# Finished w_out words left in PSUM, k and q copies on ScalarE, routing in program order

## The chip, the cores and the metric

The kernel runs on one core of one Trainium2 chip. The metric is the device time of one execution in microseconds (us); lower is better. TensorE (PE) does the matrix products, VectorE (DVE), ScalarE (ACT) and GpSimd (POOL) the elementwise work, SyncE (SP) issues most DMAs. Every engine takes its own instructions in a fixed order; engines wait for each other by semaphores.

## The reference

Three stages follow each other. `x` of one stage is the output of the stage before.

```python
# attention with a decay: 4 batches, 8 heads, 576 positions, 64 wide
scores = q @ k.T / 8 + cum[:, None] - cum[None, :]     # cum = cumsum(log f), causal
attn   = softmax(scores);  x = attn @ v                # 2304 tokens x 512
# first mixture: a dense product with a gate
h = x @ w_in                                            # 512 -> 2048
x = (h * clip(h + 3, 0, 6) / 6) @ w_out                 # 2048 -> 512
# second mixture: each token goes to one of 8 experts
e = argmax(x @ w_gate); c = softmax(x @ w_gate)[e] * sigmoid((x @ w_output_gate)[e])
out = c * (relu(x @ w1[e]) @ w2[e])                     # 512 -> 1024 -> 512
```

Inputs and output are float32.

## The kernel before

Float32 accuracy comes from pairs: every operand is split into a 16-bit high word and a 16-bit low word (`hi`, `lo`), and each product is three matmuls (hi by hi, hi by lo, lo by hi). The splits are what DVE, ACT and POOL are busy with.

**Conversion of w_in and w_out.** `w_in` and `w_out` arrive as 64-bit words. `conv_raw` (from line 638) turns 32 pieces into pairs, 16 of `w_in` ("wi") and then 16 of `w_out` ("wo"). DVE makes the float32 word in three integer operations (lines 651, 653, 655): the first two work in a PSUM tile `cv`, of which there is one, the third writes an SBUF tile `w32` (in the profile `w`), of which there are two. ACT copies it to the high word (line 658), and the low word is a subtraction (line 659), on POOL for `wi` and on DVE for `wo`.

**Attention.** A "piece" is 128 or 64 positions of several heads of k or q. `split_kq` (line 206) makes high and low words, a DMA transposes them, and a copy of the 64 high rows goes into the second operand of the score products: line 246 for k (`K2`, `K2t`), line 269 for q (`Q2`). Pieces 0 to 3 use TensorE transposes and a POOL copy instead, so the copies of lines 246 and 269 run from the fifth piece on. DVE then scales and reduces the scores (line 335, 361; `nm` is the row minimum), ACT exponentiates (369), ACT and DVE or POOL split the result (386, 387), a DMA transposes it (398), PE multiplies it with v (421 to 436), and DVE divides (444 to 462).

**First mixture.** Six chunks of 384 tokens. `moe1_steps` does the product with `w_in` (line 688), the gate (692 ACT, 695 DVE, 696 ACT, 700 DVE or POOL) and the product with `w_out` (line 711). Chunk c runs on PE between the attention units of later tokens. After each chunk `gate_steps` computes the routing of its tokens.

**The order.** Most instructions are placed by a scheduler, which simulates the engines and picks by priority; attention has priority 200 above the rest, conversions 500. Inside `tc.manual_schedule(engines=...)` the named engines keep the order of the program. In the kernel before only the last part, `round_` (line 1145 on), is in program order on PE, ACT and DVE.

**Between the two mixtures.** The tokens of experts 0 and 1 found in the first 15 blocks are gathered early, into rows that live in the freed `w_in` tile (`wi`), and `expert1` and `expert2` (lines 969 to 995) can run for them, 192 and 48 matmuls. Meanwhile the table of the remaining tokens is made: `rank_onehot` on DVE (line 931, `R`), `table` on PE (line 909, 36 matmuls) and DVE (913 to 922, `ids`), an indirect gather on POOL (943, `xg`), and a DMA transpose into `xs` (946). `round_` starts with `expert1` of expert 0 on `xs`. In `round_` the float32 weights of later experts stream in three buffers `stw` (line 859), are split by ACT (871) and DVE (872), and feed PE.

Of the kernel before, what the change touches and what calls it, by code (L numbers as in the profile page):

```python
# [11 lines left out]
I32 = mybir.dt.int32  # L12
AF = mybir.ActivationFunctionType
# [5 lines left out]
P = 128  # L19
# [39 lines left out]
def attention_moe_kernel(ctx: ExitStack, tc: tile.TileContext, q, k, v, f, w_in, w_out,  # L59
                         w_gate, w_og, w1, w2, out):  # L60
    nc = tc.nc
# [3 lines left out]
    E, _, F2 = w1.shape  # L65
# [13 lines left out]
    ps_mm = ctx.enter_context(tc.tile_pool(name="ps_mm", bufs=3, space=PSUM))  # L79
# [5 lines left out]
    stp = stage_ctx.enter_context(tc.tile_pool(name="stp", bufs=1))  # L85
# [146 lines left out]
    def prep_k(i):  # L232
        b, r, hs, (nh, n), cs = piece(i)
        if i < PE_PIECES:
            g, hh = cs.start // 256, hs.start // 4
            split_transposed("k", i, *([t[a:a + 64, hh, 2 * g + c] for c in range(2)]
                                       for t, a in ((K1, 0), (K1, 64), (K2, 0))))
            return
        src = split_kq("k", i)
        if n == 1:  # L240
            k1, k2 = K1t, K2t
        else:
            g = cs.start // 256
            k1, k2 = (t[:, hs.start // 4, 2 * g:2 * g + 2].rearrange("p c h j -> p (c h) j") for t in (K1, K2))
        nc.sync.dma_start_transpose(out=k1, in_=src)
        nc.vector.tensor_copy(out=k2[0:64], in_=k1[0:64])

    def prep_q(i):
        r = piece(i)[1]
        if i < PE_PIECES:  # L250
            q1 = ap1.tile([P, 8, 128], F16, tag="q1", name="q1", bufs=3)
            q2 = Q2[i % 3]
            q_t[i] = q1, q2
            cols = lambda t, a: [t[a:a + 64, :, c * 64:c * 64 + 64].rearrange("p (g h) j -> p g h j", g=2)
                                 for c in range(2)]
            split_transposed("q", i, cols(q2, 0), cols(q1, 0), cols(q1, 64))
            return
        src = split_kq("q", i)
        q1 = ap1.tile([P, 8, 128], F16, tag="q1", name="q1", bufs=3)
        if r == 64:  # L260
            nc.sync.dma_start_transpose(out=q1[:, :, 0:r], in_=src)
        else:
            for half in range(2):
                nc.sync.dma_start_transpose(
                    out=q1[:, half * 4:half * 4 + 4].rearrange("p h (c j) -> p (h c) j", c=2),
                    in_=src[half * 64:half * 64 + 64])
        q2 = Q2[i % 3]
        q_t[i] = q1, q2
        nc.vector.tensor_copy(out=q2[0:64, :, 0:r], in_=q1[64:128, :, 0:r])

    def q_cols(b, h, qb):

# [346 lines left out]
    WL = 2048  # L619
# [20 lines left out]
    def conv_raw(nm, i):  # L640

        if nm == "wi":
            hi, lo = (wi[:, x, :, i * P:i * P + P] for x in range(2))
        else:
            d, g4 = divmod(i, 4)
            hi, lo = (wo[:, x, 4 * g4:4 * g4 + 4, d * P:d * P + P] for x in range(2))
        w = raws.pop((nm, i)).rearrange("p (n t) -> p n t", t=2)

        t = stp.tile([P, WL // 4], I32, tag="w32", name="w32", bufs=2)
        tp = ps_cv.tile([P, WL // 4], I32, tag="cv", name="cv")  # L650
        nc.vector.tensor_scalar(out=tp, in0=w[:, :, 1], scalar1=3, scalar2=0x3FFFFFFF,
                                op0=ALU.logical_shift_left, op1=ALU.bitwise_and)
        nc.vector.scalar_tensor_tensor(out=tp, in0=w[:, :, 1], scalar=-0x40000000, in1=tp, op0=ALU.bitwise_and,
                                       op1=ALU.bitwise_or)
        nc.vector.scalar_tensor_tensor(out=t, in0=w[:, :, 0], scalar=29, in1=tp, op0=ALU.logical_shift_right,
                                       op1=ALU.bitwise_or)
        tf = t.bitcast(F32).rearrange("p (a b) -> p a b", a=4)
        last_act.append(nc.scalar.activation(out=hi, in_=tf, func=AF.Copy).ins)
        (nc.gpsimd if nm == "wi" else nc.vector).tensor_tensor(out=lo.bitcast(BF16), in0=tf, in1=hi, op=ALU.subtract)
# [219 lines left out]
    def count_rounds():  # L879

        ps = ps_mm.tile([P, 512], F32, tag="mm", name="mm")
        nc.tensor.matmul(ps[:, 0:E], lhsT=allone, rhs=ohsum[:, NB], start=True, stop=True)
        mx = mp2.tile([P, 1], F32, tag="cmx", name="cmx")
        more = mp2.tile([P, 8], F32, tag="more", name="more")
        nc.vector.tensor_reduce(out=mx, in_=ps[:, 0:E], axis=AX.X, op=ALU.max)
        nc.vector.tensor_tensor(out=more, in0=mx.to_broadcast([P, 8]), in1=thr, op=ALU.is_gt)
        nc.vector.tensor_reduce(out=mx, in_=more, axis=AX.X, op=ALU.add)
        nc.vector.tensor_copy(out=nrounds, in_=mx)
        nc.vector.tensor_copy(out=cnt, in_=ps[:, 0:E])
# [66 lines left out]
    def expert1(e, ps_pool, blocks):  # L956

        W1, (xs, o) = wts[e, 0], xs_t[e, blocks[0]]
        hT, ho = h_t[e, blocks[0]]
        w = len(blocks) * P  # L960
        hs = slice(ho, ho + w)
        for m in range(F2 // P):
            ps = ps_pool.tile([P, 512], F32, tag="mm", name="mm")
            i = 0
            for j in range(KD):
                for a, b2 in ((0, 0), (0, 1), (1, 0)):
                    l = W1[:, a, j, m * P:(m + 1) * P]
                    r = xs[:, b2 * KD + j, o:o + w]
                    nc.tensor.matmul(ps[:, 0:w], lhsT=l.bitcast(BF16) if a else l, rhs=r.bitcast(BF16) if b2 else r,  # L969
                                     start=i == 0, stop=i == 3 * KD - 1)  # L970
                    i += 1
            nc.scalar.activation(out=hT[:, m, 0, hs], in_=ps[:, 0:w], func=AF.Relu)  # L972
            nc.vector.scalar_tensor_tensor(out=hT[:, m, 1, hs].bitcast(BF16), in0=ps[:, 0:w], scalar=0.0,  # L973
                                           in1=hT[:, m, 0, hs], op0=ALU.max, op1=ALU.subtract)
            yield
# [25 lines left out]
    def run(g, n=1):  # L1001

        last = None
        for _ in range(n):
            r = next(g, "end")
            last = r or last
            if r == "end":
                break
        return last
# [121 lines left out]
            pass  # L1131
    run(wg_, 4 * KD + 1 - nw)
    count_rounds()
    for i in range(NBL, NB):
        rank_onehot(R, i, P, CAP)
    table(R, P, const, ps_mm, (1, 2), NB)

    for e in range(2):
        for _ in expert1(e, ps_mm, (0,)):
            pass  # L1140
    for e in range(2):
        for _ in expert2(e, None, ps_mm, (0,), wi[:, 1, e, 0:2 * DM].bitcast(F32)):
            pass
# [48 lines left out]
                for _ in expert2(e, xp, ps_mm, (2,)):  # L1192
                    pass

    ET = mybir.EngineType
    with tc.manual_schedule(engines={ET.PE, ET.Activation, ET.DVE}):
        round_(True)
    more = nc.values_load(nrounds[0:1, 0:1], min_val=0, max_val=NT // CAP)
    RA = xp.tile([P, NB, CAP], F16, name="RA")
    with tc.For_i(0, more, 1):  # L1200
# [35 lines left out]
```

## Time and profile before

| | us |
|---|---|
| median of 3 runs | 835.37 (833.76 to 836.37) |
| profiled execution, its own time | 831.17 |
| its span, first to last instruction | 829.5 |
| PE busy | 746.0 |
| DVE busy | 486.3 |
| ACT busy | 427.3 |
| POOL busy | 314.1 |
| mean granted TensorE clock | 0.962 of 2.4 GHz |

PE is busy for nine tenths of the span, so the span is PE's work plus the time in which PE has nothing to do or runs at the lower of its two clock levels. The readings are therefore made by stretch: how much PE idles in it, which wait ends that idle time, and how full the engine is that it waited for.

### The profile page before, as it was taken

What the parts mean: (1) busy time and instruction counts of PE and PEld (TensorE: products, weight loads), DVE (VectorE), ACT (ScalarE), POOL (GpSimd) and SP (SyncE); (2) the same over time, 40 slices, a digit from 0 to 9 for tenths busy, and PEclk for the clock granted to TensorE, in tenths of its full rate; (3) what the DMA queues carried; (4) which work ended last, traced back from release to release, by engine and by line L of the source; (5) the groups of instructions that cost most, each with busy time, mean ns of one, the idle gap of its engine ahead of it and who ended that gap; (6) DMA issues with size and microseconds to landing.
All of it is one profiled execution on the core that took longest, in us unless ns stands there. A gap on an engine that the chain in (4) does not pass through costs nothing. (4 is left out here: it accounts for less than half of the span.)

```text
span 829.5 us, 16702 instructions
## 1 busy us (share of the span) xinstructions
PE 746.0 (90%) x6166; PEld 480.1 (58%) x6177; DVE 486.3 (59%) x1302; ACT 427.3 (52%) x879; POOL 314.1 (38%) x388
## 2 busy tenths in 40 slices
PE   4745998889899989998999999999889999999993
PEld 2533455545566645665665656666769665667641
DVE  7998999838852865158723777760313555554510
ACT  4864776557754774256733655550113555454510
POOL 9546777656744463256522500000131322210010
PEclk9986999979999999998999999999899999999997
DMA  8758789999995684479623847612463899795410
GB/s 247 218 184 190 173 186 236 214 129 164 174 169 115 137 153 83 72 119 168 109 50 71 144 130 237 187 41 51 78 147 86 249 275 276 221 266 206 149 39 28
DMA packets 263779, 127.96 MB, mean 154 GB/s; under 512 B 214658, under 2 KB 247522, under 8 KB 263684
## 3 DMA queue, kind: packets, MB, share of 16 engines
q1 hardware_dynamic: 251860, 105.20, 58.1%
q0 software_dynamic: 4960, 15.73, 5.6%
q10 hardware_dynamic: 6864, 5.80, 2.5%
q8 instruction: 54, 0.88, 0.5%
q14 instruction: 41, 0.34, 0.2%
HBM read 71.52 MB, written 10.08 MB: 98 GB/s over the span
## 5 line engine op out<-in xcount | busy, mean ns | idle before, releaser
L688 PE MATMUL mm<-xT,wi 128*128 128x384 f16 (+1 forms) x1152 | 211.9, 332 | 9.1 <-DMA xT<-xn 4.9
L711 PE MATMUL mm<-g,wo 128*128 128x384 f16 (+1 forms) x1152 | 201.8, 328 | 0.4 <-DVE hr L695 0.4
L688 PEld LDWEIGHTS <-wi 128*128 128x128 f16 (+1 forms) x1152 | 111.0, 99 | 88.8 <-issue 21.5
L711 PEld LDWEIGHTS <-wo 128*128 128x128 f16 (+1 forms) x1152 | 111.7, 98 | 74.4 <-issue 3.8
L969 PEld LDWEIGHTS <-W 128*128 128x128 f16 (+1 forms) x1344 | 102.8, 101 | 15.2 <-issue 6.8
L369 ACT ACTIVATE ms<-ms,nm 128x512 f32<-128x512 f32 (+4 forms) x144 | 79.5, 579 | 55.5 <-DVE nm L335 30.5
L872 DVE TENSOR_TENSOR W<-stw,W 128x1024 bf16<-128x1024 f32 x64 | 77.7, 1224 | 50.6 <-ACT W L871 50.2
L387 POOL TENSOR_TENSOR pn<-ms,pn 128x384 bf16<-128x384 f32 (+1 forms) x80 | 83.0, 1044 | 62.2 <-ACT pn L386 53.4
L969 PE MATMUL mm<-xs,W 128*128 128x256 f16 (+3 forms) x1152 | 96.8, 246 | 5.9 <-DMA xs<-xg 3.6
L988 PE MATMUL mm<-W,hT 128*128 128x512 f16 (+1 forms) x422 | 93.8, 379 | 1.1
L871 ACT ACTIVATE W<-stw 128x1024 f16<-128x1024 f32 x64 | 66.8, 1054 | 45.4 <-DMA stw<-in_moe_w_dram 42.9
L335 DVE CUSTOM_DVE_ANT_1 ms<-sc,mask 128x128 f32<-128x128 f32 (+3 forms) x128 | 58.9, 485 | 24.6 <-PE sc L288 13.9
L988 PEld LDWEIGHTS <-hT 128*128 128x128 f16 (+1 forms) x432 | 41.9, 98 | 50.9 <-issue 1.6
L696 ACT ACTIVATE g<-hr 128x384 f16<-128x384 f32 x96 | 49.9, 520 | 41.2 <-DVE hr L695 40.6
L700 DVE TENSOR_TENSOR g<-hr,g 128x384 bf16<-128x384 f32 x80 | 53.8, 673 | 25.7 <-ACT g L696 25.5
L695 DVE SCALAR_TENSOR_TENSOR hr<-hr,mm 128x384 f32<-128x384 f32 x96 | 52.6, 548 | 16.1 <-ACT hr L692 15.4
L973 DVE SCALAR_TENSOR_TENSOR hT<-mm,hT 128x128 bf16<-128x128 f32 (+1 forms) x96 | 32.6, 355 | 47.9 <-ACT hT L972 43.3
L288 PE MATMUL sc<-K,q 128*128 128x256 f16 (+3 forms) x192 | 49.1, 300 | 12.8 <-DVE nm L335 9.1
L692 ACT ACTIVATE hr<-mm,bias 128x384 f32<-128x384 f32 x96 | 54.5, 568 | 11.5 <-PE mm L688 10.1
L995 POOL DMA_INDIRECT out_dram<-y,ids x18 | 20.1, 1115 | 96.4 <-ACT y L994 56.1
L421 PE MATMUL pv<-vt,pt 128*128 128x65 f16 x320 | 42.0, 199 | 15.6 <-DVE xs L446 9.5
L943 POOL DMA_INDIRECT xg<-rows,ids x22 | 24.9, 1130 | 70.7 <-DMA xs<-xg 63.7
(186 smaller groups left out, 1128.3 us busy)
## 6 DMA issues: line engine op xcount, KB each, us to landing
stw<-in_moe_w_dram SPq DMA_DIRECT2D x64, 512.0 KB
wo<-in_moe_w_in_dram SPq DMA_DIRECT2D x16, 512.0 KB
raw<-in_moe_w_out_dram ACTq DMA_DIRECT2D x11, 512.0 KB
rows<-rw POOLq DMA_DIRECT2D x15, 256.0 KB, 4.0
ldk<-in_k_dram SPq DMA_DIRECT2D x14, 256.0 KB
ldq<-in_q_dram SPq DMA_DIRECT2D x14, 256.0 KB
ldv<-in_v_dram SPq DMA_DIRECT2D x13, 256.0 KB
g<-in_moe_w_out_dram SPq DMA_DIRECT2D x3, 512.0 KB
```

The source lines that it names most:

```text
L335: nc.vector.tensor_tensor_reduce(out=pairs(ms[:, off:off + w]), in0=ps[:, 0:w].rearrange("p (c j) -> p c j", c=2), in1=pairs(mask[:, 640 - ...
L369: nc.scalar.activation(out=ms[:, off:off + w], in_=ms[:, off:off + w], func=AF.Exp, scale=-1.0, bias=nm[:, i:i + 1])
L387: nc.gpsimd.tensor_tensor(out=lo.bitcast(BF16), in0=ms[:, 0:N], in1=hi, op=ALU.subtract)
L688: nc.tensor.matmul(ps[:, 0:w], lhsT=l.bitcast(BF16) if a else l, rhs=r.bitcast(BF16) if b2 else r, start=i == 0, stop=i == 3 * KD - 1)
L692: nc.scalar.activation(out=hr, in_=ps[:, 0:w], func=AF.Relu, bias=bias3)
L695: nc.vector.scalar_tensor_tensor(out=hr, in0=hr, scalar=6.0, in1=ps[:, 0:w], op0=ALU.min, op1=ALU.mult)
L700: either.tensor_tensor(out=g[:, m, 1, 0:w].bitcast(BF16), in0=hr, in1=g[:, m, 0, 0:w], op=ALU.subtract)
L711: nc.tensor.matmul(ps[:, 0:w], lhsT=l.bitcast(BF16) if a else l, rhs=r.bitcast(BF16) if b2 else r, start=i == 0, stop=i == 3 * NF - 1)
L871: nc.scalar.activation(out=hi, in_=sts[i], func=AF.Copy)
L872: nc.vector.tensor_tensor(out=lo.bitcast(BF16), in0=sts[i], in1=hi, op=ALU.subtract)
L969: nc.tensor.matmul(ps[:, 0:w], lhsT=l.bitcast(BF16) if a else l, rhs=r.bitcast(BF16) if b2 else r, start=i == 0, stop=i == 3 * KD - 1)
L988: nc.tensor.matmul(ps, lhsT=l.bitcast(BF16) if a else l, rhs=r.bitcast(BF16) if b2 else r, start=i == 0, stop=i == 3 * NF2 - 1)
```

## The change

Three edits. (1) In `conv_raw`, for `w_out` only, the third DVE operation writes into the PSUM tile `cv` in place of an SBUF tile, and ACT and DVE read the finished word there. (2) The copies of lines 246 and 269 are ACT activations in place of DVE copies. (3) Program order on PE, ACT and DVE begins earlier: two steps of expert 0's first product, the one-hot rows and the table, then the rest of the first products of experts 0 and 1, their second products, and then `round_`.

```diff
-        nc.vector.tensor_copy(out=k2[0:64], in_=k1[0:64])
+        nc.scalar.activation(out=k2[0:64], in_=k1[0:64], func=AF.Copy)
...
-        nc.vector.tensor_copy(out=q2[0:64, :, 0:r], in_=q1[64:128, :, 0:r])
+        nc.scalar.activation(out=q2[0:64, :, 0:r], in_=q1[64:128, :, 0:r], func=AF.Copy)
...
-        t = stp.tile([P, WL // 4], I32, tag="w32", name="w32", bufs=2)
         tp = ps_cv.tile([P, WL // 4], I32, tag="cv", name="cv")
...
+        t = stp.tile([P, WL // 4], I32, tag="w32", name="w32", bufs=2) if nm == "wi" else tp
         nc.vector.scalar_tensor_tensor(out=t, in0=w[:, :, 0], scalar=29, in1=tp, op0=ALU.logical_shift_right,
                                        op1=ALU.bitwise_or)
...
+    ET = mybir.EngineType
+    first = [expert1(e, ps_mm, (0,)) for e in range(2)]
+    manual = ctx.enter_context(ExitStack())
+    manual.enter_context(tc.manual_schedule(engines={ET.PE, ET.Activation, ET.DVE}))
+    run(first[0], 2)
     for i in range(NBL, NB):
         rank_onehot(R, i, P, CAP)
     table(R, P, const, ps_mm, (1, 2), NB)
-    for e in range(2):
-        for _ in expert1(e, ps_mm, (0,)):
-            pass
+    for g_ in first:
+        run(g_, F2 // P)
...
-    with tc.manual_schedule(engines={ET.PE, ET.Activation, ET.DVE}):
-        round_(True)
+    round_(True)
+    manual.close()
```

The scheduler reacts to edits 1 and 2: from the first chunk on the rows of PE, DVE and ACT stand in another order. By the end of the product with `w_out` of chunk 1, the program before has issued 172 score matmuls (lines 288, 355, 356) and the changed one 202; in the middle of the product with `w_in` of chunk 3 both have issued 296.

On DVE, the second and third pieces of `w_out`. Before (`w_853` and `w_979` are two SBUF words):

```order
L653 SCALAR_TENSOR_TENSOR cv<-raw,cv 128x512
L246 COPY K2t<-K1t 64x512
L695 SCALAR_TENSOR_TENSOR hr<-hr,mm 128x384
L655 SCALAR_TENSOR_TENSOR w_853<-raw,cv 128x512
L651 TENSOR_SCALAR cv<-g 128x512
L269 COPY Q_1_89<-q_1051 64x8x64
L659 TENSOR_TENSOR wo<-w_853,wo 128x4x128
L653 SCALAR_TENSOR_TENSOR cv<-g,cv 128x512
L695 SCALAR_TENSOR_TENSOR hr<-hr,mm 128x384
L655 SCALAR_TENSOR_TENSOR w_979<-g,cv 128x512
```

And now:

```order
L652 SCALAR_TENSOR_TENSOR cv<-raw,cv 128x512
L656 SCALAR_TENSOR_TENSOR cv<-raw,cv 128x512
L696 SCALAR_TENSOR_TENSOR hr<-hr,mm 128x384
L660 TENSOR_TENSOR wo<-cv,wo 128x4x128
L650 TENSOR_SCALAR cv<-g 128x512
L696 SCALAR_TENSOR_TENSOR hr<-hr,mm 128x384
L652 SCALAR_TENSOR_TENSOR cv<-g,cv 128x512
```

The two copies are gone from DVE, and the first operation of a piece stands behind the subtraction of the piece before it, where it stood ahead of it.

On ACT, the same stretch. Before:

```order
L310 ACTIVATE vt_91<-ldv 128x8x64
L214 ACTIVATE kp<-ldk 128x8x64
L696 ACTIVATE g<-hr 128x384
L658 ACTIVATE wo<-w_853 128x4x128
L692 ACTIVATE hr<-mm,bias_86 128x384
L214 ACTIVATE qp<-ldq 128x8x64
```

And now:

```order
L310 ACTIVATE vt_91<-ldv 128x8x64
L246 ACTIVATE K2t<-K1t 64x512
L214 ACTIVATE kp<-ldk 128x8x64
L697 ACTIVATE g<-hr 128x384
L693 ACTIVATE hr<-mm,bias_86 128x384
L269 ACTIVATE Q_1_89<-q_1046 64x8x64
L214 ACTIVATE qp<-ldq 128x8x64
```

Each copy stands directly ahead of the split of the next piece (line 214).

On PE, where `round_` begins (`wi` are the early tokens, `xs` the ones gathered last). Before:

```order
L969 LDWEIGHTS W_7248
L969 MATMUL mm<-wi,W_7248 128x128
L969 LDWEIGHTS W_7129
L1183 TENSOR_LOAD cnt x8
L969 MATMUL mm<-xs_8461,W_7129 128x128
```

And now:

```order
L989 LDWEIGHTS wi
L989 MATMUL mm<-W_7637,wi 128x512
L970 LDWEIGHTS W_7113
L1188 TENSOR_LOAD cnt x8
L970 MATMUL mm<-xs_8445,W_7113 128x128
```

The first matmul on `xs` stood ahead of 48 matmuls of the first product on `wi` and of all 48 of the second product; now all 192 and 48 stand ahead of it.

## Rows read from the trace of the kernel before

**Rows 1.** The page, part 1: busy time, share of the span, instructions.

```profile
PE 746.0 (90%) x6166; PEld 480.1 (58%) x6177; DVE 486.3 (59%) x1302; ACT 427.3 (52%) x879; POOL 314.1 (38%) x388
```

**Rows 2.** Busy time by stretch. Columns: stretch, its length, then PE, PEld, DVE, ACT, POOL busy us (and instructions), the granted clock, the DMA share, GB/s.

```profile
80.00:160.00 80.00, 70.22 (x543) 42.52 (x540) 76.90 (x182) 55.62 (x118) 57.80 (x61) 0.99 0.95 204
160.00:240.00 80.00, 71.20 (x673) 44.42 (x671) 53.26 (x178) 53.63 (x120) 48.55 (x62) 0.92 0.94 158
...
280.00:420.00 140.00, 134.16 (x1108) 82.59 (x1107) 82.72 (x274) 80.23 (x182) 64.22 (x80) 0.98 0.65 116
...
620.00:829.00 209.00, 192.41 (x1575) 130.90 (x1582) 87.98 (x143) 89.98 (x162) 40.22 (x35) 0.98 0.62 179
```

**Rows 3.** PE's waits from 80 to 160 us: line waited for, total us, times, longest us.

```profile
PE sc L288 <- DVE nm L335: 4.3, 5, 1.1
PE mm L688 <- DVE hr L695: 2.5, 4, 1.0
PE pv L421 <- DVE xs L462: 1.7, 2, 1.3
```

**Rows 4.** The same from 80 to 240 us, the two that grow most.

```profile
PE sc L288 <- DVE nm L335: 6.3, 8, 1.3
...
PE pv L421 <- DVE xs L446: 2.3, 1, 2.3
```

**Rows 5.** DVE busy time from 80 to 160 us of line 246 alone, of line 269 alone, of line 659 alone (instructions, clock, DMA share, GB/s as in rows 2; line 659 has POOL as a second engine).

```profile
80.00:160.00 80.00, 4.08 (x6) 0.99 0.95 204
...
80.00:160.00 80.00, 5.23 (x6) 0.99 0.95 204
...
80.00:160.00 80.00, 18.03 (x16) 0.00 (x0) 0.99 0.95 204
```

**Rows 6.** Three DVE lines by themselves: count, shortest/median/longest ns, first and last start, shape. Line 659 and 700 subtract one SBUF tile from another, line 380 an SBUF tile from a PSUM tile.

```profile
L659 DVE TENSOR_TENSOR wo<-w,wo x16: 669/778/2959, 80.2 to 158.0; 128x512 bf16<-128x512 f32 x16
...
L700 DVE TENSOR_TENSOR g<-hr,g x80: 532/559/1632, 188.1 to 559.1; 128x384 bf16<-128x384 f32 x80
...
L380 DVE TENSOR_TENSOR pt<-mm,pt x16: 530/551/558, 28.5 to 60.6; 128x384 bf16<-128x384 f32 x16
```

**Rows 7.** The timelines of DVE and of POOL from 148 to 152 us: start, length, instruction.

```profile
148.79 2.96 DVE L659 TENSOR_TENSOR wo<-w,wo 128x512 bf16<-128x512 f32 x1
...
148.01 1.21 POOL L215 TENSOR_TENSOR qp<-ldq,qp 64x512 f16<-64x512 f32 x1
149.18 1.15 POOL L215 TENSOR_TENSOR kp<-ldk,kp 128x512 f16<-128x512 f32 x1
150.29 0.91 POOL L387 TENSOR_TENSOR pn<-ms,pn 128x384 bf16<-128x384 f32 x1
```

**Rows 8.** Groups of instructions by line: two ACT copies to 16 bits of the two widths concerned (busy us, mean ns of one, idle before).

```profile
L214 ACT ACTIVATE kp<-ldk 64x512 f16<-64x512 f32 x4 | 2.5, 632 | 5.8 <-DMA K<-kp 5.6 <-DMA ldk<-in_k_dram 0.2
...
L871 ACT ACTIVATE W<-stw 128x1024 f16<-128x1024 f32 x64 | 66.8, 1054 | 45.4 <-DMA stw<-in_moe_w_dram 42.9
```

**Rows 9.** Waits of ACT and of DVE over the whole span for the transposes of k and q.

```profile
ACT kp L214 <- DMA K<-kp: 10.4, 6, 3.4
...
DVE Q L269 <- DMA q<-qp: 13.5, 8, 3.8
```

**Rows 10.** PE's timeline between the mixtures: start, length, instructions; in brackets the idle time before and what ended it.

```profile
593.04 0.86 PE L909 MATMUL mm<-M,R 128*128 128x56 bf16 x15
593.72 2.74 PE L969 MATMUL mm<-wi,W 128*128 128x128 f16 x24
596.26 1.19 PE L909 MATMUL mm<-M,R 128*128 128x56 bf16 x21
597.26 7.56 PE L969 MATMUL mm<-wi,W 128*128 128x128 f16 x120
608.38 0.72 PE L969 MATMUL mm<-xs,W 128*128 128x128 f16 x10 [3.55 <-DMA xs<-xg]
608.93 3.80 PE L969 MATMUL mm<-wi,W 128*128 128x128 f16 x36
...
613.80 10.52 PE L988 MATMUL mm<-W,wi 128*128 128x512 f16 x47
624.16 2.01 PE L969 MATMUL mm<-xs,W 128*128 128x128 f16 x33
```

**Rows 11.** DVE's and POOL's timelines in the same place: the last one-hot row, the second low word of the first product, the indices of the table, the last write of routed rows, and the first gather.

```profile
594.13 0.28 DVE L931 TENSOR_SCALAR R<-iota,rank 128x256 f16<-128x256 f16 x1
...
596.81 0.29 DVE L973 SCALAR_TENSOR_TENSOR wi<-mm,wi 128x128 bf16<-128x128 f32 x1 [0.99 <-ACT wi L972]
...
598.00 0.17 DVE L917 CAST ids<-u 128x16 uint32<-128x16 f32 x1
...
597.18 0.54 POOL L786 DMA_DIRECT2D rows<-wi  x1 [0.61 <-DMA wi<-x]
600.75 0.99 POOL L943 DMA_INDIRECT xg<-rows,ids  x1 [3.02 <-ACT wi L972]
```

**Rows 12.** Busy time as in rows 2, of the 5.6 us behind PE's idle time there.

```profile
608.40:614.00 5.60, 5.60 (x69) 5.50 (x69) 0.87 (x3) 0.83 (x3) 2.85 (x3) 0.70 0.75 167
```

**Rows 13.** Two pieces of the chain that ended last: start, length, what.

```profile
676.09 6.76 DMA stw<-in_moe_w_dram
...
683.97 0.83 DVE W L872
```

More of the change, by code (lines that the diff above doesn't have):

```diff
@@ L1193, in round_ @@
                     pass
-    ET = mybir.EngineType
-    with tc.manual_schedule(engines={ET.PE, ET.Activation, ET.DVE}):
-        round_(True)
+    round_(True)
+    manual.close()
     more = nc.values_load(nrounds[0:1, 0:1], min_val=0, max_val=NT // CAP)
```

## The prediction

> **What bounds the kernel now.** I read the page's first part, then busy time by stretch, then PE's waits in the stretches where PE idles, and last the timelines where the third edit lies. PE is busy 746.0 of 829.5 us [rows 1], so a gain must come from the other 83.5 us or from PE's clock. The stretches that the edits touch hold these losses [rows 2]: from 80 to 160 us PE idles 80 - 70.2 = 9.8 us, from 160 to 240 us 8.8 us, from 280 to 420 us 5.8 us. From 620 us on it is busy 192.4 of 209 us, and most of the rest lies behind its last matmul.
>
> In the first of these stretches DVE is busy 76.9 of 80 us, ACT 55.6 [rows 2]: DVE is the full engine. PE's waits say the same: scores waiting for DVE's reduction to free a PSUM buffer 4.3 us, matmuls waiting for the gate 2.5, products with v waiting for DVE's division 1.7, together 8.5 of the 9.8 us [rows 3]. Up to 240 us the first of them grows to 6.3 us, and 2.3 us of another DVE division join [rows 4]. The clock in the second stretch is 0.92 [rows 2]; with 71.2 us of busy PE this costs about 0.08 x 71.2 = 5.7 us.
>
> **Edit 1, the word in PSUM.** The subtraction of `w_out` takes 18.03 us for 16 pieces, all between 80 and 160 us [rows 5]. Its shortest is 669 ns and its longest 2959 [rows 6], and the longest runs beside three POOL operations that stand back to back from 148.01 to 151.20 us [rows 7]. Line 700, also SBUF from SBUF, spreads from 532 to 1632 ns; line 380, which has the same width and reads one operand from PSUM, stays between 530 and 558 [rows 6]. So the new form should take about 0.68 us each: 18.03 - 16 x 0.68 = 7.2 us off DVE. Bounds: 0 if the long ones have another cause, 7.3 at 669 ns; I take 7.2, since line 380 is the same operation.
> The Trainium skill ("SBUF — State Buffer", the section on the shared port pair) says that a DVE operation with two SBUF inputs and a GpSimd operation hold one port pair exclusively, the loser blocking for the whole instruction. By it no subtraction of the new form can be long and the 7.2 us stand; without it they could fall to the lower bound. The three POOL rows beside the 2.96 us bear it out. The Trainium skill ("Perfetto Trace Analysis", Optimizing Scalar/DVE Operations) speaks against the edit: it puts a DVE access to PSUM about 65 ns above one to SBUF, which over 16 subtractions would be an estimated 1 us; line 380's median of 551 ns against 559 of line 700 shows none of it.
> The edit adds a wait. There is one `cv` tile, and the next piece's first operation may now start only when the subtraction has ended, which itself waits for ACT's copy; before, it was free after the third operation. A piece's chain becomes four DVE operations of 0.68 us and an ACT copy of 0.63, some 3.4 us, against 80/16 = 5.0 us in which one piece is done now. What is queued behind the waiting subtraction on DVE are the reductions and gates PE waits for. The scheduler has set attention rows between, so I take nothing; the bound is 16 x 0.63 = 10 us of DVE idle time, which would give back edit 1.
>
> **Edit 2, the copies.** DVE loses 4.08 + 5.23 = 9.3 us of copies from 80 to 160 us [rows 5]. ACT gets 32 copies. The nearest rows for their width are 632 ns at 512 columns and 1054 at 1024 [rows 8]: 24 x 1.05 + 8 x 0.63 = 30 us over the kernel, of which the 12 copies before 160 us (8 wide, 4 narrow) are 8 x 1.05 + 4 x 0.63 = 10.9 us. Bounds: if 16-bit to 16-bit were as fast as on DVE, 9.3 us; 10.9 if not; I take 10.9. The copy waits for a transposing DMA, and behind it on ACT stand exponentials and gates, for which DVE, POOL and then PE wait. DVE waited 13.5 us for q's transposes. But ACT already waits 10.4 us for k's, in line 214, which reuses the source buffer of that transpose [rows 9], and the copies stand right ahead of line 214: the wait is moved forward in the same queue, not doubled. I take nothing for it; its bound is the 13.5 us.
>
> Together, from 80 to 160 us DVE falls from 76.9 to 76.9 - 7.2 - 9.3 = 60.4 us, ACT rises from 55.6 to 66.5 us [rows 2, 5]. Neither is full any more, so I let two thirds of the 8.5 us of DVE-made waits go: 6 us. Why not all: the scheduler uses the room to bring attention forward, which refills both engines (ACT above all), and PE's order stays fixed, so every late row still stops it. For 160 to 240 us I take no change, with up to 4.3 us of waits (2.0 of the first and 2.3 of the second, [rows 3, 4]) and half of the 5.7 us of clock as what could go besides; and for 280 to 420 us none, as DVE has room there [rows 2].
>
> **Edit 3, the routing.** Before, PE runs 15 table matmuls, 24 of the first product, 21 of the table, 120 of the first product, and then idles 3.55 us for `xs`, whose matmul stands there; behind it the clock is 0.70 for 5.6 us, a mean of both levels [rows 10, 12]. 36 matmuls take 3.80 us there, 106 ns each; in steady running 33 take 2.01, 61 ns.
> After: from 593.04 us, 24 matmuls at the slow rate of now, 2.74 us, to 595.8, 0.68 us earlier than now (593.72 less 593.04). The table needs the last one-hot rows, which now follow the second low word on DVE. That one moves the 0.68 us too, from 596.81 to 596.13, and ends at 596.4; the three rows, about 0.25 us apart, end near 597.2, where they ended at 594.4 [rows 11]. The 18 to 21 table matmuls that need them take 1.1 us, to 598.3, PE having idled about 0.5 us. Then 168 matmuls at 61 ns, 10.2 us, to 608.5, and 48 of the second product as now, 624.16 - 613.80 = 10.4 us, to 618.9. The main product on `xs` starts there. Before, it stood at 624.16 with 20 of its matmuls done, worth 20 x 0.061 = 1.2, so at 623.0. Gain: 4.1 us.
> The gather is no later: the indices come near 599.0 instead of 598.0, but the first gather starts at 600.75, 3.0 us after the last write of routed rows was issued (597.18 + 0.54) [rows 11], and that is untouched. `xs` is there at 608.4, ten us before it is wanted. What follows, the weight stream, starts from DVE's and ACT's rows behind these products, in program order, so it shifts with them. Bounds: 2.0 (the table another 2.1 us late, near the 2.8 that the one-hot rows move), 5.5 (the 3.55 us, and 1.6 from 36 matmuls at 61 in place of 106 ns, and some 0.3 from the twenty on `xs`).
>
> **The sum.** 831.17 (the profiled execution, 1.7 us above its span) - 6 - 4.1 = 821.1. The median of the runs shown is 4.2 us above that execution, so the median becomes 835.4 - 10.1, rounded 825.
>
> **Rivals.**
> (A) The early stretches give nothing: the DMA engines are 0.95 and 0.94 busy there [rows 2], transposes among them, and if these set the pace, freeing DVE only moves waits. Against it: DVE ends 8.5 of 9.8 us. Then 835.4 - 4.1 = 831.3.
> (B) All early waits go, with the dull clock behind them: 8.5 + 4.3 + 2.9 = 15.7, and 4.1: 815.6. For it: DVE and ACT would both have room; against: the fixed order.
> (C) The weight stream takes the gain of edit 3. For it: in the chain that ended last, a piece's DMA takes 6.76 us, and ACT's and DVE's split of it follow, up to 683.97 [rows 13]; if its start did not shift, PE would wait later for what it gained. Then 835.4 - 6 = 829.4.
> (D) Slower: ACT becomes the wall between 80 and 160 us. With the copies it holds 66.5 of 80 us; attention brought forward by the scheduler adds to that, and from about nine tenths on, each copy that waits in ACT's queue holds exponentials and gates back, for which PE waits as it waits for DVE now. If the 10.9 us of copies then stand on PE's path in full and the DVE gain is void: 10.9 - 4.1 = +6.8, 842.2. Against it: 13.5 us of room. The Trainium skill ("Perfetto Trace Analysis", Optimizing Scalar/DVE Operations) says that moving work to ScalarE may make sense where DVE is saturated, and that an operation with a fast DVE mode is faster on DVE; by it the 20 copies from 160 us on, where DVE holds 53.3 of 80 us, are moved without need, which is this rival in a later stretch.
>
> **Chances.** Forecast 0.46, A 0.20, B 0.17, C 0.07, D 0.10. The forecast's own range is 821 to 829.5 (the early stretch from 4 to 8.5 us, edit 3 from 2.0 to 5.5: between 6 and 14 off). The range that holds 8 in 10 goes from just below B's 815.6 to past A's 831.3, towards D: 814 to 834. About 0.3%, 2.5 us, is what a measurement of this kernel can tell from no change: faster means below 832.9. Forecast, B and C lie below it, A mostly: 0.46 + 0.17 + 0.06 + 0.13 = 0.82. Within it: the rest of A and C, 0.08, and 0.01 of D. Slower: the 0.09 of D that is left.
>
> **What would show it.** Right: no stretch of 3 us without PE work between the mixtures, and the first `xs` matmuls behind both second products, near 26 us after the first matmul on `wi`; line 659's successor at 0.69 us without long ones; DVE below 65 us from 80 to 160 us in what is the same work; PE's waits for DVE there under 4 us. Wrong: PE waiting for ACT's exponentials or gates; ACT rows with idle time for transposes of k or q by more than the 10.4 us of now; DVE waiting for ACT's copy of `w_out` by more than 5 us in all; a table that ends after 600 us.

## The result and the profile after

The changed kernel takes 845.0 us (median of 4 runs, 844.3 to 847.6), the kernel before beside it 834.6 (4 runs, 833.6 to 836.4): 1.0136 times as long, 95% interval 1.0109 to 1.0163. It is slower; the prediction was 825 us. The profiled execution has a span of 845.9 us against 829.5. These two executions lie 16.4 us apart where the medians lie 10.4 apart: the one before is 3.4 us under its median, the one after 2.6 above. What is read from this pair is therefore in all some 6 us too large for a typical pair.

The page, part 1, and busy time by stretch of the changed kernel answer to [rows 1, 2] (columns as there).

```profile
PE 751.0 (89%) x6177; PEld 482.5 (57%) x6177; DVE 465.0 (55%) x1270; ACT 451.2 (53%) x911; POOL 307.2 (36%) x388
```

```profile
80.00:160.00 80.00, 70.96 (x604) 44.91 (x603) 56.96 (x163) 65.50 (x137) 58.12 (x69) 0.98 1.01 198
160.00:240.00 80.00, 64.71 (x591) 40.04 (x589) 52.17 (x179) 54.74 (x115) 43.57 (x55) 0.85 0.92 164
240.00:280.00 40.00, 34.40 (x241) 21.39 (x239) 14.65 (x38) 22.93 (x51) 20.50 (x24) 0.91 0.66 131
280.00:420.00 140.00, 133.13 (x1100) 81.71 (x1098) 74.49 (x245) 81.26 (x173) 55.06 (x67) 0.98 0.60 105
...
160.00:180.00 20.00, 9.79 (x89) 5.34 (x86) 13.86 (x37) 10.86 (x24) 10.78 (x15) 0.69 1.02 192
180.00:200.00 20.00, 17.99 (x121) 10.13 (x121) 9.18 (x30) 14.03 (x27) 11.12 (x14) 0.71 0.87 155
```

The stretch from 240 to 280 us, which the rows before do not show, was this one in the kernel before:

```profile
240.00:280.00 40.00, 40.00 (x352) 26.10 (x350) 15.98 (x49) 19.57 (x46) 17.89 (x22) 1.00 0.69 132
```

From 80 to 160 us DVE lost 20 us and ACT gained 10, near the forecast's 16.5 and 10.9, and PE's busy time did not fall: 70.96 us against 70.22. But the work in the stretch is not the same: 12 of the 16 subtractions of `w_out` are done by 160 us, where all 16 were, so part of DVE's 20 us is work that slipped behind. The loss shows behind it, from 160 to 280 us. From 160 to 240 PE is busy 64.7 us in place of 71.2, at a granted clock of 0.85 in place of 0.92, and half idle from 160 to 180; from 240 to 280 it is 34.4 us at 0.91 in place of 40.0 at 1.00.

The matmuls of the product with `w_out`, before and after (duration shortest/median/longest, first and last start):

```profile
L711 PE MATMUL mm<-g,wo x1152: 322/326/528, 122.9 to 588.7; 128*128 128x384 f16 x192
```

```profile
L712 PE MATMUL mm<-g,wo x1152: 322/326/527, 132.3 to 609.9; 128*128 128x384 f16 x192
```

The last of them, which ends the first mixture, starts at 588.7 us before and at 609.9 after: 21 us lost in front. From there to the end of the span it was 240.8 us and is 236.0: 4.8 us won behind.

DVE's subtraction of `w_out` by itself, as in [rows 6], and three of DVE's waits from 80 to 280 us:

```profile
L660 DVE TENSOR_TENSOR wo<-cv,wo x16: 681/691/693, 80.6 to 185.0; 128x512 bf16<-128x512 f32 x16
```

```profile
DVE g L701 <- ACT g L697: 14.3, 9, 3.2
DVE hr L696 <- ACT hr L693: 14.2, 17, 2.2
DVE wo L660 <- ACT wo L659: 13.6, 8, 4.3
```

Before, the first two of these waits were 3.5 and 7.1 us and the third was none. The operation became short and even, as hoped, but DVE now stands idle 13.6 us in front of it, and the last piece starts at 185.0 us in place of 158.0. The longest of these waits, in the timelines of DVE and of ACT (start, length, instruction, idle time before):

```profile
150.36 0.69 DVE L656 SCALAR_TENSOR_TENSOR cv<-raw,cv 128x512 int32<-128x512 int32 x1
155.30 0.69 DVE L660 TENSOR_TENSOR wo<-cv,wo 128x512 bf16<-128x512 f32 x1 [4.25 <-ACT wo L659]
```

```profile
150.91 0.63 ACT L246 ACTIVATE K2t<-K1t 64x512 f16<-64x512 f16 x1 [2.54 <-DMA K1t<-kp]
...
153.51 0.63 ACT L269 ACTIVATE Q<-q 64x512 f16<-64x512 f16 x1
154.15 0.63 ACT L214 ACTIVATE qp<-ldq 128x512 f16<-128x512 f32 x1
154.69 0.58 ACT L659 ACTIVATE wo<-cv 128x512 f16<-128x512 f32 x1
```

DVE has the word finished at 151.0. ACT's copy of it needs 0.58 us but stands in ACT's queue behind a copy of k, which waits 2.54 us for its transpose, and seven more rows, a copy of q among them. Until 155.3 DVE can do nothing, since the subtraction is next in its queue, and the one PSUM buffer stays taken.

While the words are late, PE has only attention, and that runs as a chain of waits. PE, DVE, POOL and ACT around 168 us:

```profile
171.06 0.61 PE L288 MATMUL sc<-K,q 128*128 128x512 f16 x1 [5.12 <-DVE nm L335]
```

```profile
170.44 0.56 DVE L335 CUSTOM_DVE_ANT_1 ms<-sc,mask 128x384 f32<-128x384 f32 x1 [3.08 <-POOL pn L387]
```

```profile
169.50 1.83 POOL L387 TENSOR_TENSOR pn<-ms,pn 128x384 bf16<-128x384 f32 x2 [3.80 <-DMA pt<-pn]
```

```profile
168.84 0.52 ACT L386 ACTIVATE pn<-ms 128x384 f16<-128x384 f32 x1 [3.84 <-DMA pt<-pn]
169.27 0.60 ACT L369 ACTIVATE ms<-ms,nm 128x384 f32<-128x384 f32 x1
...
169.78 0.51 ACT L386 ACTIVATE pn<-ms 128x384 f16<-128x384 f32 x1
170.19 0.57 ACT L659 ACTIVATE wo<-cv 128x512 f16<-128x512 f32 x1
```

Read from the top: the scores wait for DVE's reduction, DVE for POOL to free an `ms` buffer, and POOL and ACT, which both write `pn`, for a transpose that still reads the old `pn`. And a word of `w_out`, ready on DVE since 167.4, waits behind these rows on ACT until 170.19.

### The profile page after: what moved, and what is told of

Its sections match the earlier page's. It is cut to its first block, busy times and chain, and to the rows that moved or that the text cites. A ratio compares the mean times of both kernels' runs of the same rounds, so it can differ in the third digit from the quotient of the medians.

```text
span 845.9 us, 16718 instructions
## 1 busy us (share of the span) xinstructions
PE 751.0 (89%) x6177; PEld 482.5 (57%) x6177; DVE 465.0 (55%) x1270; ACT 451.2 (53%) x911; POOL 307.2 (36%) x388
## 5 line engine op out<-in xcount | busy, mean ns | idle before, releaser
L689 PEld LDWEIGHTS <-wi 128*128 128x128 f16 (+1 forms) x1152 | 111.2, 99 | 83.4 <-issue 16.6
L970 PEld LDWEIGHTS <-W 128*128 128x128 f16 (+1 forms) x1344 | 100.1, 98 | 12.4 <-issue 5.1
L701 DVE TENSOR_TENSOR g<-hr,g 128x384 bf16<-128x384 f32 x80 | 58.4, 731 | 38.5 <-ACT g L697 38.3
L335 DVE CUSTOM_DVE_ANT_1 ms<-sc,mask 128x128 f32<-128x128 f32 (+3 forms) x128 | 59.1, 485 | 26.2 <-PE sc L288 11.5
L421 PE MATMUL pv<-vt,pt 128*128 128x65 f16 x320 | 43.7, 201 | 25.3 <-DMA pt<-pn 11.2
L288 PE MATMUL sc<-K,q 128*128 128x256 f16 (+3 forms) x192 | 51.1, 315 | 14.6 <-DVE nm L335 13.2
L693 ACT ACTIVATE hr<-mm,bias 128x384 f32<-128x384 f32 x96 | 54.5, 568 | 14.1 <-PE mm L689 11.5
L722 DVE SCALAR_TENSOR_TENSOR x<-mm,x 128x384 bf16<-128x384 f32 x24 | 13.2, 555 | 78.8 <-ACT x L721 78.8
```

The source lines that it names most:

```text
L335: nc.vector.tensor_tensor_reduce(out=pairs(ms[:, off:off + w]), in0=ps[:, 0:w].rearrange("p (c j) -> p c j", c=2), in1=pairs(mask[:, 640 - ...
L693: nc.scalar.activation(out=hr, in_=ps[:, 0:w], func=AF.Relu, bias=bias3)
L701: either.tensor_tensor(out=g[:, m, 1, 0:w].bitcast(BF16), in0=hr, in1=g[:, m, 0, 0:w], op=ALU.subtract)
```

## The experiments

Ratios are to the kernel before on the same chip, with 95% intervals; 0.3% is 2.5 us.

```
edits in the kernel                         us      ratio   interval          last w_out subtraction
none (before)                               833     1                          158.0
1                    e1_word_alone          836.7   1.0041  1.0010 to 1.0073   174.7
2                    e2_copies_alone        840.3   1.0088  1.0065 to 1.0112   156.7
3                    e3_routing_alone       825.1   0.9916  0.9883 to 0.9949   159.6
2 and 3              e23_without_word       833.5   1.0017  0.9999 to 1.0035   157.1
1 and 3              e13_without_copies     828.6   0.9962  0.9937 to 0.9986   170.5
3, k's copies        e3_k_copies            834.0   1.0003  0.9974 to 1.0033   160.1
3, q's copies        e3_q_copies            828.5   0.9946  0.9913 to 0.9978   161.0
1 and 3, k's         e13_k_copies           835.0   1.0010  0.9987 to 1.0033   175.8
1 and 3, q's         e13_q_copies           826.8   0.9907  0.9872 to 0.9943   175.2
all (the change)                            845.0   1.0136  1.0109 to 1.0163   185.0
all, hi_by_dve                              834.8   1.0025  1.0005 to 1.0046   171.3
all, two_word_buffers                       838.6   1.0088  1.0052 to 1.0125   139.6
all, all_edits_other_order                  838.3   1.0080  1.0053 to 1.0107   178.9
1 and 3, e13_hi_by_dve                      833.5   1.0015  0.9991 to 1.0039   175.6
3, e3_act_load                              827.4   0.9918  0.9892 to 0.9944   162.6
3, e3_act_wait                              825.8   0.9901  0.9868 to 0.9935   159.8
3, e3_act_both                              832.8   1.0027  1.0001 to 1.0053   157.9
3, e3_k_by_pool                             840.3   1.0134  1.0075 to 1.0193   153.8
3, e3_k_left_out                            828.7   0.9976  0.9958 to 0.9995   154.7
```

**The edits one at a time.** Each kernel has the lines of the change's diff for the edits that its row names, and no others.

e1_word_alone: 

> Edit 1 alone. Theory W (one PSUM buffer makes the pieces of w_out wait for each other, DVE's next piece behind ACT's copy): the last subtraction of w_out ends past 178 us (158.0 before, 185.0 after), the products of chunk 1 end some 20 us later, the time is 842 to 856 us. Theory A (ACT's new copies are the cause): the subtraction ends within 5 us of 158, each subtraction takes 0.69 us, the time is 827 to 836 us.

e2_copies_alone: 

> Edit 2 alone. Theory W: little changes, 830 to 837 us, the last subtraction of w_out within 5 us of 158.0. Theory A: ACT's queue, held by copies that wait for transposes, delays ACT's copies of w_out and exponentials; the last subtraction past 170 us and the time 842 to 852 us.

e3_routing_alone: 

> Edit 3 alone. Both theories: nothing changes up to the last gate (last L711 or L712 matmul within 1 us of 588.7), the part behind it 4 to 5 us shorter (240.8 to 236.0 us as in the changed kernel): 829 to 832 us. If the gain behind it was only a matter of another start or clock: 833 to 836 us.

e23_without_word: 

> The changed kernel with edit 1 undone. Theory W: the 21 us lost in front come back, 826 to 833 us. Theory A: most of the loss stays, 838 to 848 us. If both share it: 833 to 838 us.

Edit 3 alone makes the kernel faster, by 0.84%, more than was expected (825.1 us against 829 to 832); edits 1 and 2 each make it slower, by 0.41 and 0.88%. The three together would be +0.45% if they added up; they are +1.36%. Neither theory holds alone: edit 1 delays the words by 17 us and costs little, edit 2 leaves them in place and costs more. With edit 1 undone more than half of the front's loss returns (1.0017): what edits 1 and 2 cost on top of edit 3 is 2.2% (1.0136 against 0.9916), of which edit 2 alone makes 1.0.

e13_without_copies: 

> The changed kernel with edit 2 undone. If the edits add up: 825.1 + 3.9 = 829 us. If edit 1 costs by itself what it costs on top of edits 2 and 3 (845.0 - 833.5 = 11.5): 836 to 837 us. Theory W says the first: without copies that wait in ACT's queue, DVE waits 7.7 us for ACT's copy of w_out, not 13.6.

Met (828.6). Edit 1 alone costs 0.46% on edit 3, so 0.7 of the 2.2% come only when edits 1 and 2 stand together. Without the copies DVE waits 5.0 us for ACT's copy of `w_out` (7.7 in e1_word_alone), with them 13.6:

```profile
DVE wo L660 <- ACT wo L659: 5.0, 5, 2.5
```

**The wait in the words' buffer.** Two changes to the whole change:

```
-        last_act.append(nc.scalar.activation(out=hi, in_=tf, func=AF.Copy).ins)
+        if nm == "wi":
+            last_act.append(nc.scalar.activation(out=hi, in_=tf, func=AF.Copy).ins)
+        else:
+            nc.vector.tensor_copy(out=hi, in_=tf)
```

hi_by_dve: 

> The changed kernel with the high copy of w_out on DVE, so that no piece waits for ACT. Theory W (pieces wait in the one PSUM buffer for ACT's copy, which stands behind copies that wait for transposes): DVE's 13.6 us of waiting for that copy are gone, DVE has 16 x 0.62 = 10 us more work, the last subtraction falls from 185 to 165 to 172 us, the time from 845 to 834 to 840 us. Rival S (the one buffer alone does it, whoever makes the copy): the last subtraction stays past 178 us, the time 841 to 849 us.

```
-    ps_sc = attn_ctx.enter_context(tc.tile_pool(name="ps_sc", bufs=3, space=PSUM))
+    ps_sc = attn_ctx.enter_context(tc.tile_pool(name="ps_sc", bufs=2, space=PSUM))
-    ps_cv = stage_ctx.enter_context(tc.tile_pool(name="ps_cv", bufs=1, space=PSUM))
+    ps_cv = stage_ctx.enter_context(tc.tile_pool(name="ps_cv", bufs=2, space=PSUM))
```

two_word_buffers: 

> The changed kernel with two PSUM buffers for the words and two in place of three for the scores. Theory W: a piece can start while the last one waits for ACT; the last subtraction near 160 to 168 us, the time 830 to 838 us, less what the third buffer of the scores was worth. Rival O (ACT's load with the copies is what counts, the buffer is not): 841 to 850 us, the last subtraction past 175 us.

The first meets theory W (834.8 us, 171.3) and takes back 1.1 of the 1.36% although DVE has 16 operations more. That the words' wait behind ACT's queue was a cost in the whole change is likely by this, but the edit also gave the scheduler another list; how much of the 1.1 that may be is seen below, under the order. With two buffers the words are done at 139.6 us, 45 us earlier and earlier than any theory had it, and the time is only 0.5% better (838.6, just past theory W's range), with a score buffer given up for it: early words alone do not make a fast kernel. The same move on edits 1 and 3:

e13_hi_by_dve: 

> Edits 1 and 3 with the high copy of w_out on DVE. If what edit 1 costs without the copies (828.6 - 825.1 = 3.5 us) is the wait for ACT's copy (5.0 us of DVE): 825 to 827 us, the last subtraction near 165 us. If it is the one buffer whoever copies: 828 to 831 us, the last subtraction near 170.

A miss on both sides: 833.5, 0.5% slower than with ACT's copy, and the words are later, 175.6 against 170.5 us. Without edit 2 the copy by ACT is held up less, and DVE, which now makes 16 copies of 0.68 us, is the full engine again. Busy time by stretch, of this kernel and then of edits 1 and 3:

```profile
80.00:160.00 80.00, 71.64 (x564) 44.20 (x563) 75.12 (x181) 48.17 (x103) 54.08 (x61) 0.96 0.97 196
```

```profile
80.00:160.00 80.00, 73.48 (x615) 45.85 (x613) 67.67 (x182) 57.27 (x126) 59.34 (x69) 0.98 1.01 210
```

**Which copies.**

e3_k_copies: 

> Routing in program order, and of the copies those of k alone by ACT. If the cost of edit 2 goes with ACT's waits for transposes (k 5.7, q 6.4 us of 12.1): 829 us, half of the 8 us between 825.1 and 833.5. If q's copies alone do it: 824 to 827. If k's alone: 832 to 835.

e3_q_copies: 

> Routing in program order, and of the copies those of q alone by ACT. If the parts of edit 2 add up: k's alone cost 834.0 - 825.1 = 8.9 us of the 8.4 of both, so q's cost nothing, 823 to 827 us. If either kind alone throws ACT's queue out of step: 831 to 835 us.

e13_q_copies: 

> Edits 1 and 3, and of the copies those of q alone by ACT. If the parts add up: 828 to 830 us, as without copies (828.6). If any copy that waits for a transpose in ACT's queue holds up the words in their one buffer: 833 to 840 us, the last subtraction past 176 us.

e13_k_copies: 

> Edits 1 and 3, and of the copies those of k alone by ACT. If k's copies and edit 1 together make the loss whatever q does: 841 to 847 us, like the whole change, the last subtraction past 178 us. If the parts add up (0.38% under before, and 0.87% for k's copies): 835 to 838 us. If it takes both kinds of copies in ACT's queue to hold up the words: 830 to 835 us.

On edit 3, k's copies cost 0.87% (834.0 us, the case of k's alone) and q's 0.30 (828.5, between the two ranges), the second no more than the intervals allow. On edits 1 and 3, q's copies cost nothing (0.9907 against 0.9962; 826.8 us, below both ranges) and k's 0.48% (835.0, as if it added up). Only both kinds together with edit 1 reach 1.36%. DVE's wait for ACT's copy of `w_out` goes the same way: 5.0 us with q's copies, 4.2 with k's, 13.6 with both. Late words are not the price by themselves: in e13_q_copies they are some 16 us later than in edit 3 alone (175.2 against 159.6), PE is half idle from 160 to 180 us (11.6 us at a clock of 0.61), and the kernel is no slower than edit 3 alone. The whole change differs from it further on: from 160 to 280 us its PE is busy 99.1 us, in e13_q_copies 107.0, before 111.2.

**What k's copies cost by.** All on edit 3 alone; in the first three k's own copy stays on DVE, and `scr` is room that nobody reads (its definition is not shown; e3_k_left_out also clears `K2t` once on POOL at the start):

```
+        for x in range(2):                                     # e3_act_load
+            nc.scalar.activation(out=scr[:, x * 512:x * 512 + 512].rearrange("p (n d) -> p n d", d=D),
+                                 in_=src.rearrange("p (n c d) -> p n c d", c=2, d=D)[0:32, :, 0], func=AF.Copy)
+        nc.scalar.activation(out=scr[0:64, 0:8], in_=k1[0:64, 0:8, 0], func=AF.Copy)      # e3_act_wait
+        nc.scalar.activation(out=scr.rearrange("p (n j) -> p n j", n=8)[:, :, 0:k1.shape[2]],
+                             in_=k1[64:96], func=AF.Copy)                                 # e3_act_both
-        nc.vector.tensor_copy(out=k2[0:64], in_=k1[0:64])
+        nc.gpsimd.tensor_copy(out=k2[0:64], in_=k1[0:64])                                 # e3_k_by_pool
+        nc.vector.tensor_copy(out=k2[0:64, 0:1], in_=k1[0:64, 0:1])                       # e3_k_left_out
```

e3_act_load: 

> Routing in program order; the copies stay on DVE, and ACT gets, where k's copy would stand, two copies of 512 columns that nobody reads and that wait for no transpose (about 2 x 0.62 = 1.24 us, the copy of k takes 1.05). Theory L (k's copies cost ACT's time): 832 to 836 us. Theory D (they cost because ACT waits for the transpose in front of exponentials): 824 to 827 us.

e3_act_wait: 

> Routing in program order; the copies stay on DVE, and ACT gets, where k's copy would stand, a copy of 8 columns of the transposed k that nobody reads: the wait without the time. Theory D: 831 to 835 us, with ACT's waits for k's transposes ahead of it. Theory L: 824 to 827 us.

e3_act_both: 

> Routing in program order; k's copy stays on DVE, and ACT makes one of the same width from the same transposed rows, in front of it, that nobody reads: time and wait together on ACT, nothing off DVE. Theory J (time and wait together cost k's 8.9 us): 831 to 836 us. Theory R (it is the copy's leaving DVE, by the rows that the scheduler then places otherwise): 824 to 828 us.

e3_k_by_pool: 

> Routing in program order; k's copies by POOL, so that DVE loses them and ACT's queue is as before. Theory J: 822 to 827 us. Theory R: 830 to 836 us. By POOL's own load of some 20 copies of a microsecond or more it could also be slower, with POOL's subtractions of the exponentials waited for: 829 to 835 us, and then DVE's waits for POOL rise above 6.2 us.

e3_k_left_out: 

> Routing in program order; of k's second copy only one row in eight is written by DVE, the rest is left out (the scores then use stale rows), so that DVE loses most of it and nobody gains it. Theory J: 822 to 826 us. Theory R: 829 to 835 us, though nobody has more to do.

Neither ACT's time (32 copies of 0.63 us) nor ACT's wait alone (9.3 us in front of 16 copies of 0.2 us) costs anything (0.9918 and 0.9901 against 0.9916): theories L and D both fail. Time and wait in one instruction cost 1.1%, with nothing taken off DVE. ACT's waits from 80 to 280 us, in edit 3 alone and then in e3_act_both (lines two higher there):

```profile
ACT pn L386 <- DMA pt<-pn: 11.4, 13, 2.5
```

```profile
ACT pn L388 <- DMA pt<-pn: 18.6, 11, 6.0
```

So attention's own loop, from exponentials to `pn` to transposes, has ACT wait 7 us longer there, and the same wait is 15.3 us in e3_k_copies and 14.9 in e2_copies_alone. That it is the price is not shown: it is 14.1 us in e3_act_load too, which lost nothing, and 11.5 in the whole change, which lost most. Nor is it shown that time and wait together are the cause: in e3_act_both ACT waits only 3.1 us in front of the added copies, and the rows stand in another order (264 score matmuls ahead of the end of the second product with `w_out`, where edit 3 alone and e3_act_wait have 256). Leaving most of k's copy out, which gives ACT and DVE nothing more to do, costs 0.6% too (828.7 us, between the ranges of J and R), and on POOL, where it takes 1.03 us and POOL waits 8.6 us for transposes, 2.2% (840.3 us, above every range given). What k's copies cost on edit 3 (0.87%) is thus less than the sum of the two parts (1.1 and 0.6), and how it divides between ACT's queue and the order that the scheduler writes for the new list stays open.

**The order.** The kernels with edit 1 that lack a kind of copy have 190 score matmuls ahead of the end of the first product with `w_out` in PE's program order (before: 172); the whole change has 202. One constant gives all three edits an order with 190:

```
-LEAD = 2
+LEAD = 1
```

all_edits_other_order: 

> All three edits, and attention is asked for one step earlier in the first product of chunk 1 (a lead of 1 step in place of 2), which leaves the work as it is and gives the scheduler another list: 190 score matmuls stand ahead of the end of the first product with w_out, as in the kernels with edit 1 that lack one kind of copy, in place of 202. Theory O (the last 1.3 percent of the whole change is the order that the scheduler gave it): 833 to 839 us. Theory Q (ACT's queue with both kinds of copies and edit 1's words does it in any order): 843 to 848 us, the last subtraction of w_out past 180 us.

838.3 us, near the upper end of theory O's range: another order of the same work is worth some 0.56% of the 1.36 (the intervals, 1.0109 to 1.0163 and 1.0053 to 1.0107, just stand apart). Whether the same constant would also move the kernel before, or edit 3 alone, was not run. The kernel hi_by_dve has 190 score matmuls at that place too, so part of its 1.1% may be the order; but it lies another 0.55% below this one (1.0025 against 1.0080, intervals apart), and that much goes to taking the copy of `w_out` off ACT, if one takes the like count as a like order (the two differ again in the second product, 264 against 272). The rest stays here, and so do the signs of it, DVE's wait for ACT's copy of `w_out` first:

```profile
L660 DVE TENSOR_TENSOR wo<-cv,wo x16: 671/691/692, 79.2 to 178.9; 128x512 bf16<-128x512 f32 x16
its engine sat idle before it (us, times) until:
  ACT wo L659: 11.3, 5
```

```profile
160.00:180.00 20.00, 10.33 (x98) 5.85 (x97) 15.09 (x44) 12.49 (x30) 11.17 (x16) 0.63 0.97 173
```

PE is half idle from 160 to 180 us here too, by the stretch's row. No version of the front was measurably faster than the one before; edit 3 alone, 825.1 us, beats both kernels.

## Why the prediction was wrong

The prediction counted 6 us won by edits 1 and 2; on top of edit 3 they cost 2.2%, some 18 us. Two waits that it put at nothing are the steps that failed.

**Edit 1's subtraction: right.** 691 ns and none long, where 0.68 us was the term; about 7 us left DVE (18.0 us for 16 before, 11.0 after). The Trainium skill ("SBUF — State Buffer", Who interferes with whom) has a DVE instruction with two SBUF inputs contend with a GpSimd instruction that reads SBUF, the one that issues second being blocked until the first has finished; the runs agree with what follows from it, since the form with one PSUM input never stretches (700 ns at most) and the other did in every kernel that has it (1185 ns or more at the longest). The Trainium skill ("Perfetto Trace Analysis", Optimizing Scalar/DVE Operations) puts DVE's access to PSUM about 65 ns above that to SBUF; the shortest subtractions, 669 to 681 ns with the PSUM input and 659 to 678 without, show 22 ns at the most.

**Edit 1's wait: the first step that failed.** "I take nothing; the bound is 16 x 0.63 = 10 us." DVE waited 13.6 us, past the bound. The bound took ACT's copy at its own length; its price is the length of ACT's queue in front of it, 4.25 us in the timeline shown. Pieces 5.0 us apart with a chain of 3.4 looked safe, but the chain now holds what another engine does in between. Where ACT's queue was free of the copies, the wait was 5.0 us and edit 1 cost 0.46% on edit 3: less than the bound, and still no gain. A wait of more than 5 us there is one of the signs by which the prediction said it would be wrong.

**Edit 2: durations right, the zero for the wait wrong.** ACT's copies take 1052 and 621 ns against the 1054 and 632 taken, and ACT's load from 80 to 160 us is 65.5 us against 66.5. The claim that the wait for the transposes is only moved forward, not doubled, holds: over all of ACT's rows from 80 to 280 us it sums to 12.7 us before and 12.1 after. But "I take nothing for it" does not follow: with the copies moved, the kernel was 0.88% slower alone and 1.0% on edit 3. The copy added to ACT with DVE's kept cost 1.1%, and there and with edit 2 alone it is another wait of ACT's, for attention's transposes, that grew (11.4 us in edit 3 alone, 18.6 and 14.9). What the price is made of, ACT's queue or the new order, stays open.

**"Let two thirds of the 8.5 us of DVE-made waits go": they went and others came.** PE's waits from 80 to 160 us, as in [rows 3]:

```profile
PE pv L433 <- DMA pt<-pn: 5.4, 2, 4.3
PE pv L421 <- DMA pt<-pn: 2.0, 2, 1.6
PE sc L288 <- DVE nm L335: 1.0, 1, 1.0
PE mm L689 <- DVE hr L696: 0.5, 1, 0.5
```

DVE's part fell from 8.5 to under 2 us; 7.4 us of waits for the transposes of attention's weights stand in its place. That is rival A as far as it says that freeing DVE only moves the wait, but its price was put at zero; that the DMA engines set the pace was not tested.

**160 to 240 us "no change": the largest miss.** PE has attention alone there for a while, since the words are late: 6.5 us of PE time and 0.07 of clock lost, and another 5.6 us and 0.09 of clock from 240 to 280 us, a stretch that the prediction did not look at. Late words alone do not make this loss, as e13_q_copies shows.

**Edit 3: right, and under-sized alone.** From the first mixture's last matmul to the main product on `xs` it was 623.0 - 588.7 = 34.3 us by the prediction's count. PE's timeline after:

```profile
614.25 2.16 PE L970 MATMUL mm<-wi,W 128*128 128x128 f16 x24
616.20 0.91 PE L910 MATMUL mm<-M,R 128*128 128x56 bf16 x15
617.30 1.31 PE L910 MATMUL mm<-M,R 128*128 128x56 bf16 x21 [0.19 <-DVE R L932]
618.45 8.25 PE L970 MATMUL mm<-wi,W 128*128 128x128 f16 x144
627.26 0.83 PE L970 MATMUL mm<-wi,W 128*128 128x128 f16 x12 [0.56 <-issue]
628.73 0.83 PE L970 MATMUL mm<-wi,W 128*128 128x128 f16 x12 [0.64 <-DVE wi L974]
...
640.02 12.16 PE L970 MATMUL mm<-xs,W 128*128 128x128 f16 x212
```

640.0 - 609.9 = 30.1: 4.2 us won, 4.1 forecast; the 3.55 us of idle time are gone and the table waits 0.2 us for its rows. In edit 3 alone the same row starts at 616.81 behind a last matmul at 588.2, 5.7 us won, and to the end of the span 240.8 us fall to 234.0: past the upper bound of 5.5. Most of the 1.5 us between the two kernels is PE's idle time in the first product, 0.56 and 0.64 us here; in edit 3 alone the same 168 matmuls run in one piece of 9.59 us, where the sum took 10.2. That 4.2 meets 4.1 in the changed kernel is thus in part luck. Where the last microsecond, behind the start on `xs`, lies was not followed.

**The rivals.** D had the sign: ACT at nine tenths (18.5 of 20 us from 120 to 140 us) and copies holding back what PE waits for. Its price, 10.9 us, was ACT's added time, and that its 842.2 us is near 845.0 is luck: in e3_act_load such time alone cost nothing, and in e3_act_wait the wait alone cost nothing either. What cost was the copies' move as a whole, the one buffer with it, and the order. Its chance of 0.10 rested on "13.5 us of room", a busy share, which says nothing of the queue.

## What to carry to other kernels

A buffer held across a second engine can be as slow as that engine's queue, not as its instruction (here 4.25 us for a copy of 0.58): before giving up the free copy between two engines, read what stands in front of the second engine's row and what that waits for. A busy share does not price the move of an operation that waits for a DMA: k's copies cost 0.87% on ACT and 2.2% on POOL, both with room, though on ACT neither such a time nor such a wait cost anything by itself. When a static order is written from a program's list, an edit in a full stretch buys its own effect and a new order: of the sixteen kernels here with edit 3 and something more in the front none was measurably faster than edit 3 alone, while the edit in a stretch with one plain idle time gave what was counted and more.

## What was not expected of the hardware

The same copy of 64x1024 from 16 to 16 bits takes 419 ns on DVE (median, kernel before), 1052 on ACT and 1029 on POOL: moving it costs two and a half times its length on either. DVE's subtraction from SBUF stretched to 4.46 us in the kernels with edit 2 and without edit 1, where its median was 692 and 687 ns, while the form that reads PSUM stayed between 669 and 693 ns in every kernel that has it, save one row of 700 where the words have two buffers. ACT's copy of 128x512 takes 578 ns from PSUM and 625 from SBUF (means, changed kernel), and one of 8 columns 0.2 us.
